# Holding four DMA transposes behind a load, and the next batch's loads behind the last transpose

## The chip, the cores and the metric

The kernel runs on one core of one Trainium2 chip. The metric is the device time of one execution in microseconds (us), and a kernel's figure is the median of its runs. "PE" is the tensor engine, "DVE" the vector engine, "ACT" the scalar engine, "POOL" and "SP" the two engines that issue the DMAs of this part.

## The reference, cut to what matters

Linear attention over 8 batches, whose result feeds a mixture of experts. Only the attention's first steps matter here:

```python
def phi(x, c, s):
    r = np.maximum(x, 0.0)
    return np.concatenate([r * c, r * s], axis=-1)
q_p = phi(q, cos_w, sin_w)                 # q, k, v: 8 batches, 8 heads, 576 x 64
k_p = phi(k, cos_w, sin_w)
kv = np.einsum('bhsf,bhsd->bhfd', k_p, v)  # summed over the sequence
z = np.sum(k_p, axis=2)
num = np.einsum('bhsf,bhfd->bhsd', q_p, kv)
den = np.einsum('bhsf,bhf->bhs', q_p, z)[..., None] + 1e-06
attn = num / den                           # then the experts: relu(x @ w1) @ w2, weighted
```

`q_p` must stand the other way round for its matmuls, so it is transposed. That is what the change is about.

## The kernel before

Block j runs the first expert's matmuls (`h_ps`, `y_ps`) on the j-th slice of 512 tokens and, between them, prepares later batches. Each batch's q, k and v come in six loads of 288 KB (two halves of each), issued by POOL. Heads go in four pairs. The q of batches 2 and up is multiplied by DVE into a buffer `q_p` and turned by a DMA transpose on SP's queue. Batches count from 0, so the fourth is `b == 3` and the fifth `b == 4`.

```python
te, ve, se = bound    # PE, DVE and ACT, each held to the order in which the program is written
qp_pool = p1.enter_context(tc.tile_pool(name="qp_pool", bufs=3))       # three buffers for q_p
...
def load(b, half, names="qkv", held_back=False):
    for name in names:
        x = ld.tile([P, 2, C, D], F16, name=f"{name}_ld")
        view = ...
        i = nc.gpsimd.dma_start(out=..., in_=view[:, 2 * half : 2 * half + 2])
        if held_back:
            after(ve.last, i)             # wait for DVE's last instruction so far
        landing[name, b, half] = i
...
def prep_q(b, hk):
    q16 = loaded.pop(("q", b, hk))
    by_dma = b >= 2
    if by_dma:
        ve.tensor_scalar(out=q16, in0=q16, scalar1=0.0, scalar2=None, op0=ALU.max)
    q_p = qp_pool.tile([P, C, 2, D], F16, name="q_p")
    ve.tensor_tensor(out=q_p[:], in0=..., in1=cs, op=ALU.mult)
    if by_dma:
        qTs[b, hk] = q_pTs[(b * HK + hk) % len(q_pTs)]
        turned = nc.sync.dma_start(out=qTs[b, hk], in_=..., transpose=True)
        if b == 3 and hk == 0:
            after(landing["v", b, 1], turned)
...
# block 1 prepares batch 3, block 2 batch 4; the numbers are slots of the block
(4, prep_q, 0), (5, prep_q, 1), (8, prep_k, 0), (8, prep_q, 2), ...    # j == 1
(4, prep_q, 0), (5, prep_k, 0), (5, prep_q, 1), (6, prep_k, 1),        # j == 2
(8, prep_q, 2), (8, prep_k, 2), (10, prep_q, 3), (10, prep_k, 3),
(11, prep_kv, 0), (14, prep_kv, 1),
...
if j == 1:
    for name in "qkv":
        for half in range(2):
            at(j, 12, load, b + 2, half, name, True)
```

(The comment lines are mine. In the last part `b` is j + 1, the batch whose attention block j finishes, so that block 1 prepares batch 3 and issues the loads of batch 4, the fifth, which block 2 prepares. `prep_k` is ACT's relu on k; `prep_kv` is DVE's multiplication into `k_p` and its copy of v.) The destinations of the four transposes are `q_pT`, `q_pT`, `acc_lo` and `acc_hi` in the profile, for pairs 0 to 3.

The softmax here doesn't subtract the row's maximum and nothing guards it: scores larger than these inputs give would overflow.

## Time and profile before

| before | value |
|---|---|
| median of 3 runs | 978.64 us (978.47 to 978.7) |
| span of the profiled run | 977.2 us |
| PE busy | 98% of the span |
| PE idle, 54.63 to 110.35 us | 2.00 us |
| fourth batch's transposes issued at | 54.33 (pair 1), 64.13 (0), 65.53 (2), 67.03 (3) |
| fifth batch's loads begin at | 66.92 us |

The timeline of SP's queue in the kernel before: start, length of the issuing, line, then output<-input and how many were grouped. A line with x2 or x4 covers that many transposes from the first one's start to the last one's issue; it is not their time in flight.

```profile
54.33 11.09 SPq L361 DMA_TRANSPOSE q_pT<-q_p  x2
65.53 1.32 SPq L361 DMA_TRANSPOSE acc_lo<-q_p  x1
67.03 1.48 SPq L361 DMA_TRANSPOSE acc_hi<-q_p  x1
77.75 7.20 SPq L361 DMA_TRANSPOSE q_pT<-q_p  x4
```

The first line holds pair 1 (54.33) and pair 0 (64.13, when v had landed). Then POOL's timeline in the same kernel, where the brackets say what ended POOL's wait:

```profile
66.92 1.43 POOL L202 DMA_DIRECT2D q_ld<-in_q_dram  x2 [11.63 <-DVE acc_lo L109]
```

The fifth batch's loads start a tenth of a microsecond before the transpose of pair 3 is issued at 67.03: these two meet.

### The profile page before, as it was taken

The numbers are of one execution on the slowest core, as the hardware profiler recorded it, in microseconds if no ns is written. First come the engines' busy times: TensorE is split into PE (matmuls) and PEld (weight loads), VectorE is DVE, ScalarE is ACT, GpSimd is POOL, SyncE is SP. The second block draws the span as 40 slices with busy tenths as digits, with TensorE's granted clock in tenths as the row PEclk, the third lists the DMA queues.
The fourth block names the chain that finished last, engine by engine and source line by source line (L and its number), as shares of the span: only waits on it lengthen the run. The fifth ranks groups of instructions, "written<-read, shape, count | busy, mean of one in ns | idle before, by whom it ended". The sixth has DMA issues, their size and how long they took to land.

```text
span 977.2 us, 20236 instructions
## 1 busy us (share of the span) xinstructions
PE 962.4 (98%) x7855; PEld 675.7 (69%) x7855; DVE 807.8 (83%) x1833; ACT 564.7 (58%) x1262; POOL 60.6 (6%) x82
## 2 busy tenths in 40 slices
PE   9999999999999999999999999999999999999997
PEld 6545555457777777777777777777777777777775
DVE  6767775888988887988888887988888888988887
ACT  5766665477776555555555555555555555555551
POOL 6231110010000000000000000000000000000001
PEclk9999999999999999999999999999999999999999
DMA  9999986330104401323104401323103401104435
GB/s 163 183 149 178 152 141 111 68 68 34 42 25 83 78 25 41 64 51 70 35 25 83 78 25 36 68 55 66 37 25 80 81 25 38 37 26 120 127 89 128
DMA packets 80336, 73.54 MB, mean 75 GB/s; under 512 B 33264, under 2 KB 72176, under 8 KB 80240
## 3 DMA queue, kind: packets, MB, share of 16 engines
q0 software_dynamic: 27232, 30.94, 20.3%
q1 hardware_dynamic: 52768, 41.06, 17.2%
q8 instruction: 61, 1.00, 0.4%
q14 instruction: 35, 0.29, 0.1%
q10 hardware_dynamic: 240, 0.26, 0.1%
HBM read 83.12 MB, written 12.98 MB: 98 GB/s over the span
## 4 chain that ended last, share of the span: by engine, by line
PE 88%; DMA 4%; DVE 3%; issue 2%; ACT 1%; POOL 1%; POOLq 0%; ACTq 0%; SPq 0%
PE rows_ps L109 33%; PE h_ps L109 26%; PE p_ps L109 11%; PE copied_ps L109 11%; PE y_ps L109 4%; PE small_ps L109 2%; DMA k_ld<-in_k_dram 1%; DMA w1e<-in_moe_w_dram 1%; DMA w2e<-in_moe_w_dram 1%; DMA acc_hi<-q_p 1%; DVE P_tok L109 1%; DVE colp L109 0%; POOL q_ld L202 0%; DVE rs L109 0%; DVE acc_hi L955 0%
## 5 line engine op out<-in xcount | busy, mean ns | idle before, releaser
L955 DVE SCALAR_TENSOR_TENSOR acc_lo<-rows_ps,P_tok,acc_lo 128x512 f32<-128x512 f32 (+1 forms) x322 | 203.9, 643 | 74.9 <-PE rows_ps L109 74.8
L109 PEld LDWEIGHTS <-H 128*128 128x128 f16 x2080 | 203.2, 98 | 82.5 <-issue 1.2
L891 ACT CAST u<-h_ps 128x384 f16<-128x384 f32 x288 | 138.0, 479 | 131.0 <-PE h_ps L109 131.0
L109 PEld LDWEIGHTS <-w1e 128*128 128x128 f16 x1632 | 157.7, 98 | 67.6 <-issue 5.3
L885 DVE CUSTOM_DVE_ANT_0 H<-p_ps,u 128x384 f16<-128x384 f32 x329 | 181.9, 553 | 6.5 <-PE p_ps L109 6.5
L109 PEld LDWEIGHTS <-hs 128*128 128x128 f16 x1500 | 146.6, 98 | 56.2
L109 PE MATMUL h_ps<-S,w1e 128*128 128x384 f16 x672 | 164.1, 326 | 0.7 <-ACT u L109 0.6
L109 PE MATMUL p_ps<-xT,T 128*128 128x384 f16 x672 | 164.1, 326 | 0.1
L109 PE MATMUL rows_ps<-V,H 128*128 128x256 f16 x1000 | 150.0, 273 | 0.7 <-DVE acc_hi L955 0.7
L109 PE MATMUL rows_ps<-w2e,hs 128*128 128x256 f16 x1000 | 150.0, 273 | 0.0
L109 PE MATMUL h_ps<-xT,w1e 128*128 128x384 f16 (+1 forms) x616 | 148.7, 350 | 0.1
L923 ACT ACTIVATE H<-h_ps 128x384 f16<-128x384 f32 x144 | 70.8, 492 | 95.0 <-PE h_ps L109 95.0
L109 PEld LDWEIGHTS <-T 128*128 128x128 f16 x1008 | 98.4, 98 | 30.2 <-issue 3.6
L109 PE MATMUL rows_ps<-w2e,H 128*128 128x256 f16 (+1 forms) x568 | 92.3, 285 | 0.0
L904 ACT COPY copied_ps<-h_ps 128x384 f32<-128x384 f32 x144 | 67.5, 469 | 35.4 <-PE h_ps L109 35.4
L914 ACT ACTIVATE H<-copied_ps 128x384 f16<-128x384 f32 x144 | 71.0, 493 | 20.3 <-PE copied_ps L109 20.3
L109 PE MATMUL h_ps<-S,T 128*128 128x384 f16 x336 | 81.8, 325 | 0.4 <-ACT copied_ps L109 0.3
L109 PE MATMUL copied_ps<-xT,w1e 128*128 128x384 f16 x336 | 82.1, 326 | 0.0
L109 PE MATMUL copied_ps<-w2e,H 128*128 128x256 f16 x504 | 75.5, 272 | 0.0
L109 PE MATMUL rows_ps<-V,hs 128*128 128x256 f16 x500 | 75.0, 272 | 0.0
L955 DVE SCALAR_TENSOR_TENSOR acc_lo<-copied_ps,P_tok,acc_lo 128x256 f32<-128x256 f32 x126 | 60.4, 480 | 0.6 <-PE copied_ps L109 0.2
L955 DVE SCALAR_TENSOR_TENSOR acc_hi<-rows_ps,P_tok,acc_hi 128x512 f32<-128x512 f32 (+1 forms) x56 | 41.4, 739 | 20.5 <-PE rows_ps L109 19.7
(145 smaller groups left out, 951.7 us busy)
## 6 DMA issues: line engine op xcount, KB each, us to landing
S<-x_saved SPq DMA_DIRECT2D x108, 192.0 KB, 2.4
out_dram<-acc_lo SPq DMA_DIRECT2D x62, 128.0 KB, 2.4
w1e<-in_moe_w_dram POOLq DMA_DIRECT2D x7, 1024.0 KB, 8.8
w2e<-in_moe_w_dram POOLq DMA_DIRECT2D x7, 1024.0 KB, 9.7
q_ld<-in_q_dram POOLq DMA_DIRECT2D x16, 288.0 KB, 7.1
k_ld<-in_k_dram POOLq DMA_DIRECT2D x16, 288.0 KB, 8.5
v_ld<-in_v_dram POOLq DMA_DIRECT2D x16, 288.0 KB, 9.6
x_saved<-S SPq DMA_DIRECT2D x18, 192.0 KB, 1.9
```

The costliest lines, as they stand in the source:

```text
L109: i = getattr(self.engine, name)(*args, **kwargs)
L885: latest = ve._custom_dve(TENSOR_ADD_SAT, out=out, in0=ps[:, 0:TU], in1=t[:], s0=FP32_MAX, s1=0.0)
L891: se.copy(out=t[:], in_=ps[:, 0:TU])
L904: se.copy(out=Y[:, 0:TU], in_=X[:, 0:TU])
L914: se.activation(out=h11, in_=Y[:, 0:TU], func=AF.Relu)
L923: se.activation(out=h12, in_=X[:, 0:TU], func=AF.Relu)
L955: ve.scalar_tensor_tensor(out=a, in0=rows, scalar=P_tok[:, g, self.e : self.e + 1], in1=a, op0=ALU.mult, op1=ALU.add,)
```

## The change

The intent: keep transposes and loads of one batch apart, and the next batch's loads off the last transpose. It also moves the fifth batch's k relus later, to leave the loads time.

```diff
-        def load(b, half, names="qkv", held_back=False):
+        def load(b, half, names="qkv", held_back=False, behind=None):
...
-                if held_back:
+                if behind is not None:
+                    after(turnings[behind], i)
+                elif held_back:
                     after(ve.last, i)
...
-                if b == 3 and hk == 0:
+                if b == 3:
                     after(landing["v", b, 1], turned)
+                turnings[b, hk] = turned
...
-                    (4, prep_q, 0), (5, prep_k, 0), (5, prep_q, 1), (6, prep_k, 1),
-                    (8, prep_q, 2), (8, prep_k, 2), (10, prep_q, 3), (10, prep_k, 3),
+                    (4, prep_q, 0), (5, prep_q, 1), (7, prep_k, 0), (8, prep_k, 1),
+                    (8, prep_q, 2), (9, prep_k, 2), (10, prep_q, 3), (10, prep_k, 3),
...
-                        at(j, 12, load, b + 2, half, name, True)
+                        at(j, 12, load, b + 2, half, name, True, (b + 1, HK - 1))
```

More of the change, by code (lines that the diff above doesn't have):

```diff
@@ L195 @@
         landing = {}
+        turnings = {}
         sources = {"q": q, "k": k, "v": v}
-        def load(b, half, names="qkv", held_back=False):
+        def load(b, half, names="qkv", held_back=False, behind=None):
             for name in names:
```

## The prediction

> **What bounds the kernel now.** I read the share of each engine first, then the slices, then the tensor engine's (PE's) waits in the stretch that the change touches, then the orders of time there.
>
> ```profile
> PE 962.4 (98%) x7855; PEld 675.7 (69%) x7855; DVE 807.8 (83%) x1833; ACT 564.7 (58%) x1262; POOL 60.6 (6%) x82
> ...
> PE   9999999999999999999999999999999999999997
> ```
>
> PE is busy 98% of the span and in nearly every slice, so a change counts only by what it adds to or takes from PE's idle time. The change touches the batches around 50 to 90 us. The table by stretches gives PE 17.30 us busy of the 19.30 us from 54.6 to 73.9, and no idle from 73.9 to 88. So about 2.0 us of idle time is all there is to win here, 0.2% of 978.64. PE's waits from 36 to 160 us name the larger pieces:
>
> ```profile
> PE small_ps L109 <- DMA acc_hi<-q_p: 1.0, 1, 1.0
> PE small_ps L109 <- ACT rb L109: 0.4, 1, 0.4
> PE small_ps L109 <- DVE acc_lo L109: 0.3, 1, 0.3
> PE small_ps L109 <- DVE k_p L109: 0.2, 1, 0.2
> ```
>
> The first is the fourth batch's last transpose (its q goes into acc_hi). It is what the change aims at. The timeline of PE shows the place, with the idle time in brackets:
>
> ```profile
> 68.43 0.46 PE L109 MATMUL small_ps<-acc_lo,k_p 64*128 64x65 f16 x18 [0.33 <-DVE acc_lo L109]
> 69.09 0.46 PE L109 MATMUL small_ps<-acc_lo,k_p 64*128 64x65 f16 x18 [0.21 <-DVE k_p L109]
> 69.48 2.76 PE L109 MATMUL h_ps<-xT,w1e 128*128 128x512 f16 x12
> 72.18 0.51 PE L109 MATMUL small_ps<-q_pT,zsel 128*32 128x192 f16 x12
> 72.52 0.34 PE L109 MATMUL small_ps<-acc_lo,zsel 128*32 128x192 f16 x6
> 73.81 0.34 PE L109 MATMUL small_ps<-acc_hi,zsel 128*32 128x192 f16 x6 [0.96 <-DMA acc_hi<-q_p]
> ```
>
> The reader is to see two things: the 0.96 us, and that the two waits just before it are for the vector engine (DVE), so at 68 to 69 us PE goes as DVE goes.
>
> **What the Trainium skill says.** "DMA: Bandwidth & Descriptors", section "Issuing engines are not separate DMA queues", says that transfers share the same 16 DMA engines and interleave, whoever issued them. This trace agrees: a transpose of 54.33 us, beside five loads, took 10.4 us to land; one of 64.13, just after the last of them landed, took 3.3; one of 67.03, beside the fifth batch's loads, took 6.7. The same page, section "Anatomy of one DMA", says that DMA engines do not wait on semaphores; the issuing sequencer does, before dispatch. So a wait holds up everything behind it on that queue; the trace shows the SP queue held 6.8 us in total by the v load. The same page's "Rules for kernel authors" says that a transpose next to ordinary DMAs needs nothing, so the new waits are for time alone.
>
> **The change, part by part.** The instruction lists of the two builds show the same order on PE and DVE in this stretch. Only three things differ.
>
> First, the order of the fourth batch's transposes. Before, only that of head pair 0 waited for the v load, so the scheduler put pair 1 ahead of it: pair 1 went at 54.33 among the loads, pair 0 at 64.13, when v landed. Now all four go after that landing, in the order 0, 1, 2, 3. The q_p pool has three buffers, so the multiplication that makes q_p of pair 3 must wait for the first finished transpose. DVE's wait is on the same semaphore lane in both builds, but that lane was pair 1's transpose and becomes pair 0's. Before:
>
> ```profile
> 63.83 0.30 DVE L109 TENSOR_SCALAR q_ld<-q_ld 128x576 f16<-128x576 f16 x1
> 64.82 0.76 DVE L109 TENSOR_TENSOR q_p<-q_ld,acc_hi 128x1152 f16<-128x1152 f16 x1 [0.70 <-DMA q_pT<-q_p]
> 65.50 0.75 DVE L109 TENSOR_TENSOR k_p<-k_ld,acc_hi 128x1152 f16<-128x1152 f16 x1
> 66.17 0.45 DVE L109 COPY acc_lo<-v_ld 128x576 f16<-128x576 f16 x1
> ```
>
> 54.33 + 10.4 = 64.7, and q_p starts at 64.82.
>
> When does it start now? The last v load was issued at 54.57 (the second of the two at 53.86, 0.72 later) and took 9.5 us: 64.1. Without the transpose among them the loads should finish earlier. Two undisturbed sets of six loads say how much: of those begun at 103.70 and 122.64 the fifth landed 11.6 and 11.1 us after the first issue; here five took 64.1 - 51.72 = 12.4. So I take 51.72 + 11.3 = 63.0 for v's landing. A transpose with no load beside it lands in 3.2 to 3.3 us even when others follow at once (those of 97.60, 99.00 and 100.44 did). So pair 0 lands at 63.0 + 0.1 + 3.3 = 66.4 and q_p of pair 3 starts at about 66.5, **1.7 us later** than 64.82.
>
> DVE keeps a fixed order, so the k_p and v copies behind it move by 1.7 us too. The second half of the key-value sums waited for exactly these (0.33 and 0.21 us above). So PE's restart at 69.48 moves to about 71.2. An earlier PE doesn't help: the new delay is set by v's landing.
>
> Second, the collision goes. q_p of pair 3 is done at about 67.2, its transpose goes at about 67.3 and, with the loads held back, lands at about 70.6. PE reaches it at about 72.8 + 1.7 = 74.5: no wait. This wins the 0.96 us.
>
> Third, the fifth batch's loads start at about 70.6 in place of 66.92, 3.7 us later. With the undisturbed spacing (5.2 us for the first, then about 1.5 each) they land at about 75.8, 77.3, 78.9, 80.4, 82.0 and 83.6, perhaps a microsecond later at the end, as that batch's own transposes come among them. Wanted: q first half by DVE at 76.60 + 0.7 = 77.3, second half at 79.3. The k relus on ACT took place from 77.25; the change puts them two or three slots later, at about 80.2 and 83, which is after 78.9 and 80.4. The v copies were at 84.20 and later, now about 84.9, after 82 to 83. So I expect these loads hidden. The moved relus free two h_ps evictions ahead of them but put 0.7 us before the second rb copy; there I allow 0 to 0.3 us of PE waiting.
>
> Sum: + 1.7 (DVE held by the buffer) - 0.96 (the collision) + 0 to 0.3 = about + 0.8; I take **+0.7 us**, as some of the DVE delay may be caught between two PE groups. 978.64 + 0.7 = 979.3. From 78 us on PE has no idle time of note up to the end of the attention part to absorb either sign, so I let it reach the end whole.
>
> **Rivals.** (a) *The collision is all that matters*: the transpose is ready in time, and q_p of pair 3 isn't late, as the v load comes far sooner without the transpose in its way. For it: k second half landed 3.0 us after k first half in before (57.8, 60.8), against about 1.5 in the undisturbed sets, so the transpose may have cost 1.5 us; v would land at 62.6, and if 62.0 the shift is 0.7 and the net -0.3. At best all 2.0 us of idle go: 976.7. Against it: the pool's buffer and 3.3 us of transpose stay. (b) *The late loads become the bound*: moved 3.7 us, with transposes among them as at 77.75 (5.0 us to land), one q, k or v misses its slot, holds DVE or ACT and then PE by 1 to 2 us: 980.5 to 981.5. For it: before, ACT already waited 0.53 us for k at 77.25. Against it: the relus were moved for this. (c) *No difference*: the wait for the transpose is exchanged for an equal one for DVE, 978.6.
>
> **Range and chances.** The term of the widest spread is v's landing, 62.0 to 64.1: the shift on DVE is then 0.7 to 2.8, the net -0.3 to +1.8. With rival (b) above it and a few tenths of spread between runs, 977.8 to 980.8 should hold 8 in 10, with the centre at 979.3. Two per cent is 19.6 us; even all the idle time of this stretch is 2.0, and no loads can be late by so much. So within 2% is near certain.
>
> **What would show it.** Right: the first transpose of the fourth batch goes at about 63 and lands 3.3 us later; DVE starts q_p of pair 3 at 66 to 67, with a wait of 2 us or more for the transpose; PE waits about 2 us in total for the k_p and v copies at 67 to 71 us; the wait for acc_hi is gone, and its transpose takes 3.3 in place of 6.7; the six loads start at about 70.6. Wrong: v lands before 62, so that DVE isn't later and the time falls below 978; or PE or ACT waits at 76 to 88 for q, k or v of the fifth batch or for rb, which would make it slower than said; or a later batch's order of transfers changes, which I take as unmoved but shifted.

## The result, and the profile after

| | before | after |
|---|---|---|
| median, 4 runs each | 978.56 us (977.54 to 978.7) | 980.23 us (979.34 to 981.58) |
| span of the profiled run | 977.2 us | 978.4 us |
| granted clock in it | 1.000 | 0.999 |

The ratio is 1.002, with a 95% interval of 1.0003 to 1.0038: within 2%, and a little slower.

PE's waits from 36 to 160 us in the changed kernel (what waited, for what: sum in us, times, longest):

```profile
PE small_ps L109 <- DVE acc_lo L109: 2.1, 3, 1.6
PE small_ps L109 <- ACT rb L109: 0.9, 1, 0.9
PE small_ps L109 <- DVE k_p L109: 0.2, 1, 0.2
```

The wait for `acc_hi`, 0.96 us before, is gone. In its place PE waits 2.1 us for DVE's v copies (`acc_lo`), where it waited 0.3. PE's timeline shows the place:

```profile
68.98 0.46 PE L109 MATMUL small_ps<-acc_lo,k_p 64*128 64x65 f16 x18 [1.62 <-DVE acc_lo L109]
...
70.74 0.46 PE L109 MATMUL small_ps<-acc_lo,k_p 64*128 64x65 f16 x18 [0.33 <-DVE acc_lo L109]
71.40 0.46 PE L109 MATMUL small_ps<-acc_lo,k_p 64*128 64x65 f16 x18 [0.21 <-DVE k_p L109]
71.79 2.76 PE L109 MATMUL h_ps<-xT,w1e 128*128 128x512 f16 x12
...
74.99 0.34 PE L109 MATMUL small_ps<-acc_hi,zsel 128*32 128x192 f16 x6
75.26 1.90 PE L109 MATMUL h_ps<-xT,w1e 128*128 128x512 f16 x8
```

The first line is the new idle time, 1.62 us. The group at 71.79 is the one that started at 69.48 before, so PE is 2.31 us late here. The `acc_hi` group at 74.99 follows without a wait, which gives 0.96 back and a little more: the group at 75.26 started at 74.09 before, so 1.17 us stays. That is nearly the whole difference of the two spans, 1.2 us. DVE's timeline says why PE waited:

```profile
67.14 0.76 DVE L109 TENSOR_TENSOR q_p<-q_ld,acc_hi 128x1152 f16<-128x1152 f16 x1 [2.44 <-DMA q_pT<-q_p]
67.81 0.75 DVE L109 TENSOR_TENSOR k_p<-k_ld,acc_hi 128x1152 f16<-128x1152 f16 x1
68.48 0.45 DVE L109 COPY acc_lo<-v_ld 128x576 f16<-128x576 f16 x1
```

DVE stood still for 2.44 us before it could fill the last `q_p`: the first line's bracket names a transpose. Its k_p and v follow in the written order, and PE's idle time ends when the first v copy is done. SP's queue shows the transposes that DVE waited for:

```profile
63.73 2.73 SPq L365 DMA_TRANSPOSE q_pT<-q_p  x2
66.56 1.35 SPq L365 DMA_TRANSPOSE acc_lo<-q_p  x1
68.08 1.28 SPq L365 DMA_TRANSPOSE acc_hi<-q_p  x1
78.93 9.18 SPq L365 DMA_TRANSPOSE q_pT<-q_p  x4
```

All four now go after v's landing; each of them landed 3.2 to 3.3 us after its issue, where that of `acc_hi` took 6.7 before. The last line holds the fifth batch's four, which took 7.0, 6.7, 5.4 and 4.3 us to land, against 5.0, 4.9, 3.8 and 4.9 before. POOL's line is the gate at work, 4.9 us after where the loads started before:

```profile
71.83 1.43 POOL L203 DMA_DIRECT2D q_ld<-in_q_dram  x2 [16.48 <-DMA acc_hi<-q_p]
```

One more measure helps from here on, because single runs spread by more than the effect. Every build issues the same PE instructions in the same order, so I take two of them, the last `h_ps` group before 55 us and an `h_ps` pair at about 110 us, and call the time between them the stretch. PE's idle time in it is the stretch less PE's busy time there. For the changed kernel the stretch is 57.16 us, of which 53.80 busy and 3.36 idle; before it is 55.72, of which 53.72 busy and 2.00 idle. After the stretch the changed kernel is shorter, 866.54 us against 866.87. The idle time leaves out a little of each wait: the `h_ps` matmul before a wait is counted as busy for its whole 0.38 us, where the next one otherwise starts 0.22 us after it. So the stretch is the safer of the two measures.

### The profile page after: what moved, and what is told of

The parts are those of the page before. It is cut to its first block, busy times and chain, and to the rows that moved or that the text cites. A ratio compares the mean times of both kernels' runs of the same rounds, so it can differ in the third digit from the quotient of the medians.

```text
span 978.4 us, 20236 instructions
## 1 busy us (share of the span) xinstructions
PE 962.3 (98%) x7855; PEld 675.6 (69%) x7855; DVE 807.7 (83%) x1833; ACT 564.3 (58%) x1262; POOL 60.6 (6%) x82
## 4 chain that ended last, share of the span: by engine, by line
PE 88%; DMA 4%; DVE 4%; issue 2%; ACT 1%; POOL 1%; POOLq 0%; DVEq 0%; ACTq 0%; SPq 0%
PE rows_ps L109 33%; PE h_ps L109 26%; PE p_ps L109 11%; PE copied_ps L109 11%; PE y_ps L109 4%; PE small_ps L109 2%; DMA k_ld<-in_k_dram 1%; DMA w2e<-in_moe_w_dram 1%; DMA w1e<-in_moe_w_dram 1%; DVE P_tok L109 1%; DVE k_p L109 0%; DVE colp L109 0%; DVE acc_lo L109 0%; DMA q_pT<-q_p 0%; DVE xT L109 0%
```

## The experiments

Theory A, my prediction's: the change wins the collision's 0.96 us and pays for it with DVE, which the three `q_p` buffers hold until the first transpose has landed. Rival B: the late loads cost time later on. The prediction's rival (a), that the collision is all that matters, is already out: the changed kernel's trace has no collision, and it isn't faster. The experiments ran in three sets of four kernels, each set on one chip; every set has 11 runs of the kernel before, with medians 979.82, 978.86 and 978.94 us.

| kernel | median (range), us | ratio to before [95%] | stretch | PE idle in it |
|---|---|---|---|---|
| the change, first runs | 980.23 (979.34–981.58) | 1.0020 [1.0003, 1.0038] | 57.16 | 3.36 |
| e1 change again | 979.87 (979.44–981.04) | 0.9999 [0.9977, 1.0021] | 56.60 | 2.65 |
| e9 change, third time | 980.68 (978.99–980.86) | 1.0010 [0.9998, 1.0022] | 57.88 | 3.71 |
| e5 before again | 978.53 (977.62–979.38) | 0.9994 [0.9979, 1.0008] | 55.67 | 1.98 |
| e2 loads gated only | 979.38 (979.00–980.07) | 0.9992 [0.9972, 1.0011] | 57.52 | 3.41 |
| e3 transposes wait only | 978.68 (978.15–979.26) | 0.9984 [0.9965, 1.0004] | 57.36 | 2.48 |
| e4 change, four buffers | 986.81 (985.53–989.58) | 1.0069 [1.0047, 1.0091] | 65.04 | 9.67 |
| e6 e2, k relus later | 979.18 (978.85–981.25) | 1.0005 [0.9989, 1.0020] | 56.70 | 2.79 |
| e7 e6, other k relu later too | 980.22 (979.69–980.73) | 1.0011 [0.9996, 1.0025] | 57.86 | 3.88 |
| e8 before, one k relu later | 978.22 (977.91–981.53) | 0.9997 [0.9980, 1.0014] | 55.15 | 1.49 |
| e10 change, k relus not moved | 980.92 (979.72–983.16) | 1.0021 [1.0008, 1.0034] | 60.79 | 4.81 |
| e11 loads behind pair 2 | 978.04 (976.57–978.87) | 0.9985 [0.9973, 0.9997] | 55.49 | 1.31 |
| e12 e11, one k relu later | 977.98 (977.51–979.06) | 0.9989 [0.9977, 1.0000] | 56.47 | 2.51 |

### e1 and e9: the change again

No edit.

> The changed kernel once more, with five rounds, to fix the size of the difference. Theory A (the wait of q_p's third buffer for the first transpose holds DVE, and PE behind it, for about 2.2 us, and 1.0 us is won back from the collision): slower by 1.0 to 1.5 us, as the profiled PE waits say (3.07 against 1.87 us). Rival C (the difference of the two medians, 1.7 us, is chance between runs): within 0.5 us of the kernel before.

> The changed kernel a third time, beside the kernel before on the same chip, since the second set left the size open (the kernel before had several runs at a lower clock there). From the traces, PE takes 55.7 us in the kernel before and 56.6 to 57.2 in the changed one between the same two of its instructions (its last h_ps group before 55 us and the pair at 110 us), and as long in both for all the rest. Expected: slower by 0.8 to 1.5 us in the medians. If the difference were chance: within 0.3 us.

In e1 the median is the same as before's, 979.87 against 979.82, though the trace is like the first one: PE waits 1.58, 0.33 and 0.21 us for DVE, and the stretch is 0.9 us longer than the 55.7 of the kernel before. The kernel before lost runs in this set: four of its eleven took 981.2 to 984.2 us. So the ratio of that set says little, and I read e1 from its trace. In e9, on another chip, the medians differ by 1.7 us, and a second cost appears. DVE's timeline, then PE's, of e9:

```profile
86.62 0.76 DVE L109 TENSOR_TENSOR q_p<-q_ld,acc_hi 128x1152 f16<-128x1152 f16 x1 [4.02 <-DMA q_pT<-q_p]
```

```profile
88.92 0.38 PE L109 MATMUL h_ps<-xT,w1e 128*128 128x512 f16 x1 [0.89 <-DVE xT L109]
89.65 0.59 PE L109 MATMUL h_ps<-xT,w1e 128*128 128x512 f16 x2 [0.35 <-DVE xT L109]
```

DVE waited 4.02 us for the fifth batch's first transpose, again for a `q_p` buffer, and PE waited 1.24 us for DVE's `xT` behind it. In the first trace the same wait of DVE was 2.33 us and cost PE nothing. This is rival B, in a form that I hadn't named: not a late load, but late loads that now run beside the fifth batch's transposes.

### e2: only the loads wait

```diff
-                if b == 3:
+                if b == 3 and hk == 0:
```

> Only the fifth batch's loads wait for the last transpose; of the fourth batch's transposes only the first waits for v, as in the kernel before (so the scheduler puts the second ahead again). Theory A: DVE isn't held (q_p of pair 3 at about 64.8), the last transpose lands in 3.3 us, PE's wait for it (0.96 us) is gone: faster than the kernel before by 0.9 to 1.1 us. Rival B (it is the late start of the fifth batch's loads that costs): still slower than the kernel before by about 1 us, as the loads still start some 3.5 us later.

The first half came as expected: the last transpose took 3.2 us, PE didn't wait for it, and DVE filled the last `q_p` at 64.82 after a wait of 0.73 us, where it had been 0.70 before. But the gain was lost: 3.41 us idle in place of 2.00. Part of it is 1.24 us for `rb` at 59.37, a wait that comes and goes (e5 below). The rest is in ACT's timeline and in PE's:

```profile
79.60 0.68 ACT L109 ACTIVATE k_ld<-k_ld 128x576 f16<-128x576 f16 x1 [1.40 <-DMA k_ld<-in_k_dram]
```

```profile
80.70 0.49 PE L109 MATMUL small_ps<-q_pT,kv_sb 128*64 128x384 f16 x4 [1.13 <-ACT rb L109]
```

ACT waited 1.40 us for k, the `rb` copy stood behind that relu, and PE waited 1.13 us for `rb`. The loads had started at 70.82. So theory A's number for this run, faster by the collision's microsecond, missed, although its reading of DVE held: gating the loads behind the last transpose costs later about what it wins, and that is rival B.

### e3: only the transposes wait

```diff
-                        at(j, 12, load, b + 2, half, name, True, (b + 1, HK - 1))
+                        at(j, 12, load, b + 2, half, name, True)
```

> All of the fourth batch's transposes wait for v, and the fifth batch's loads go when they did before (after DVE's last work). Theory A: the same DVE hold of about 2.3 us as with the whole change, so slower than the kernel before by 1.0 to 1.5 us; the last transpose and the loads collide again (over 5 us to land), but PE, late by 2.3 us, comes to it at about 75 and waits little, 0 to 0.5 us. Rival B: the loads aren't late, so no slower than the kernel before, within 0.3 us.

Here DVE's hold is alone (2.62 us before `q_p` at 65.54, PE waiting 1.79 and 0.30), and I expected the collision to stay on top of it. It didn't: the transpose of pair 3, issued at 66.56, landed in 3.3 us, as the loads started only at 67.64. They wait for a DVE copy, and DVE was late. So once all four transposes wait for v, the gate on the loads has nothing left to prevent; it only makes them later. The fifth batch's transposes took 3.2 to 4.2 us here, against 4.3 to 7.0 in the change. The time is 1.2 us under that of e1 in the same set, and not above that of the kernel before (0.9984). So theory A's number, slower by 1.0 to 1.5 us, missed, and rival B's, no slower, came true, though DVE's hold is in the trace as theory A has it.

The profiled run of e3 lost something else. PE's timeline, then the table by stretches, whose columns are the stretch, its length, then the engines' busy times in the order PE, PEld (weight loads), DVE, ACT and POOL with counts, the granted clock, the DMA share and GB/s:

```profile
67.39 0.46 PE L109 MATMUL small_ps<-acc_lo,k_p 64*128 64x65 f16 x18 [1.79 <-DVE acc_lo L109]
...
69.15 1.34 PE L109 MATMUL small_ps<-acc_lo,k_p 64*128 64x65 f16 x36 [0.30 <-DVE acc_lo L109]
70.42 3.56 PE L109 MATMUL h_ps<-xT,w1e 128*128 128x512 f16 x12
```

```profile
67.00:68.00 1.00, 0.61 (x19) 0.54 (x20) 1.00 (x4) 0.13 (x1) 0.36 (x1) 1.00 1.00 189
68.00:69.00 1.00, 0.84 (x4) 0.20 (x2) 1.00 (x3) 0.36 (x3) 1.00 (x2) 0.83 1.10 207
...
70.00:71.00 1.00, 1.00 (x20) 0.61 (x15) 0.20 (x3) 0.43 (x2) 1.00 (x2) 0.50 1.14 128
...
73.00:74.00 1.00, 1.00 (x8) 0.34 (x9) 0.00 (x0) 0.60 (x1) 0.00 (x0) 1.00 1.20 204
```

The clock fell to 0.50 at about 68.7, 1.3 us after the gap of 1.79 us had ended and before that of 0.30, and stayed there for about 3.4 us (0.83 in the stretch from 68 to 69, 0.50 from 69 to 72). The twelve matmuls at 70.42 took 3.56 us, where the same group took 2.76. The Trainium skill ("TensorE: Matmul & The Clock Gate", Part 1) says that the clock is halved after an idle window of about 3.4 us, and that this window is free-running. The trace agrees on the half, and the clock stayed halved for 3.4 us here and again in e10. It differs on the idle time: one gap of 1.79 us came before the fall here, and gaps of 1.18 and 0.67 us in e10, while the changed kernel's like gaps, 1.62 and 0.33 us, and one of 1.87 us in e7 left the clock at 1.00. What decides it is not shown.

### e4: the change with four q_p buffers

```diff
-        qp_pool = p1.enter_context(tc.tile_pool(name="qp_pool", bufs=3))
+        qp_pool = p1.enter_context(tc.tile_pool(name="qp_pool", bufs=4))
...
-        rb_pool = p1.enter_context(tc.tile_pool(name="rb_pool", bufs=4))
+        rb_pool = p1.enter_context(tc.tile_pool(name="rb_pool", bufs=3))
```

The second edit frees the memory for the first.

> The whole change, with a fourth q_p buffer (its space is taken from the rb pool, three buffers in place of four). Theory A: DVE's wait of 2.44 us for the transpose is gone, PE doesn't wait for the v copies for 1.62 us, and the collision is gone too: faster than the kernel before by 0.7 to 1.5 us, and than the changed one by about 2 us or more. Rival B: as slow as the changed kernel.

The table by stretches for 64 to 74 us, e4 and then the change:

```profile
64.00:74.00 10.00, 10.00 (x136) 5.02 (x134) 6.55 (x17) 6.09 (x15) 3.24 (x5) 1.00 0.79 137
```

```profile
64.00:74.00 10.00, 7.85 (x105) 3.92 (x104) 5.55 (x15) 5.11 (x13) 2.17 (x4) 1.00 0.71 125
```

PE is busy 10.00 us of 10 where in the change it is 7.85, with the transposes still waiting for v. So DVE's hold in the change is the buffer's, as theory A has it. But the time missed what was expected: the whole is 7 us slower than e1, from a place that nobody had asked about. PE's timeline of e4:

```profile
94.06 0.34 PE L109 MATMUL small_ps<-q_pT,zsel 128*32 128x192 f16 x6 [1.31 <-DMA q_pT<-q_p]
101.04 0.51 PE L109 MATMUL small_ps<-q_pT,zsel 128*32 128x192 f16 x6 [6.64 <-DMA q_pT<-q_p]
```

PE waits 8.0 us for the fifth batch's transposes, which took 8.7, 6.9, 10.5 and 15.5 us. In e4 DVE doesn't wait for a buffer at 81.17 either, so the sixth batch's loads, which wait for DVE, start at 83.27 in place of 88.11, among those transposes. The three buffers had held the loads back. That is shown by these traces for e4; what `rb`'s smaller pool adds wasn't tried alone (PE's waits for `rb` are 1.6 us there).

### e5 and e8: the kernel before again, and with one relu moved

e5 has no edit. e8, against before, moves one k relu of the fourth batch a slot on (and another with it):

```diff
-                    (4, prep_q, 0), (5, prep_q, 1), (8, prep_k, 0), (8, prep_q, 2),
-                    (9, prep_k, 1), (10, prep_kv, 0), (10, prep_k, 2), (12, prep_q, 3),
+                    (4, prep_q, 0), (5, prep_q, 1), (8, prep_q, 2), (9, prep_k, 0),
+                    (10, prep_k, 1), (10, prep_kv, 0), (10, prep_k, 2), (12, prep_q, 3),
```

> The kernel before against itself, to see how far it spreads and whether its slow runs have a cause in the trace. In the last set its runs went from 977.9 to 984.2 us, those above 981 all with a mean granted clock of 0.998. Theory D (short idle gaps of PE close together now and then make the throttle halve PE's clock for some 3.4 us, which costs about 1.7 us; seen once, in the run with the transposes' waits alone): again two clusters, 978 and about 2 us above, with lower mean clock in the upper one; ratio within 0.997 to 1.003. Rival (chip or order of runs): one cluster, or clusters that the clock doesn't tell apart.

> The kernel before with nothing but the fourth batch's first k relu one slot later. It takes the rb wait at 59 us away (0.4 us in the first trace). Expected: 0 to 0.5 us faster than before in its lower cluster, since from 64 us on the last transpose's landing (67.03 + 6.7) sets PE's restart and PE would only come to it earlier. If the rb wait counted in full: 0.4 to 1.2 us faster.

e5 has the waits of the kernel before: 0.92 us for `acc_hi`, whose transpose took 6.7 us again, and 0.91 for `rb` (0.4 in the first trace). So the wait for `acc_hi` repeats, and that for `rb` differs by half a microsecond between two traces of one kernel. Theory D's two clusters did not come again: e5's five runs lie within 1.8 us. Of all runs of the kernel before in the three sets, the six above 981 us had a mean clock of 0.998, but 979.69 and 979.38 us came with 0.997. No trace of one of the six was kept, so what makes them slow stays open. e8 takes the `rb` wait away and shortens the stretch by 0.5 us. The ratio, 0.9997 with an interval of 0.0034, can't confirm so little.

### e6, e7 and e12: moving relus out of the way

e6 is e2 with the fifth batch's k relus a slot later; e7 adds e8's edit to e6; e12 adds it to e11.

```diff
-                    (4, prep_q, 0), (5, prep_q, 1), (7, prep_k, 0), (8, prep_k, 1),
-                    (8, prep_q, 2), (9, prep_k, 2), (10, prep_q, 3), (10, prep_k, 3),
+                    (4, prep_q, 0), (5, prep_q, 1), (8, prep_q, 2), (8, prep_k, 0),
+                    (9, prep_k, 1), (10, prep_q, 3), (10, prep_k, 2), (10, prep_k, 3),
```

> Only the fifth batch's loads wait (as in the second experiment), but the fifth batch's k relus on ACT go one slot later still, behind the second pair's rb copies. In the second experiment PE waited 1.13 us there for rb, because ACT had waited 1.40 us for k. If the late loads were what ate the gain there: this wait is below 0.3 us, and the time is 0.8 to 1.2 us below the second experiment's, near 978.3. If not: the same as the second experiment, about 979.4.

> As the sixth, and the fourth batch's first k relu goes one slot later as well, behind the rb copies of its own slot, since PE waited 0.4 to 1.2 us for rb at 59 us whenever k landed late. Expected: that wait is 0 to 0.2 us; in all PE waits 0.6 to 0.9 us from 36 to 165 us, against 1.9 in the kernel before, and the time is 977.0 to 978.0, faster than both kernels. It fails if the k and v work that now comes later holds the sums at 66 to 70 us.

> The eleventh with the fourth batch's first k relu one slot later (as in the eighth, where it shortened the stretch by 0.5 us). Expected: 0.8 to 1.4 us below the kernel before; if the two gains don't add up, because DVE then sets the restart at 69 us, about as the eighth alone, 0.5 us below.

e6 and e7 missed their times. In e6 ACT waited 0.23 us for k in place of 1.40 and PE's second `rb` wait was gone, but DVE then waited 4.70 us for the fifth batch's first transpose (9.0 us in flight), and PE 1.62 and 0.35 us for `xT`. In e7 it was 4.95 on DVE and 1.87 and 0.35 on PE; in e12 4.07, and 0.94 and 0.35. The late loads overlap the fifth batch's transposes, and an earlier PE only meets them sooner. The median of e12 is 0.96 us below that of the kernel before in its set, inside the 0.8 to 1.4 expected, and its trace is that of the slowest of its five runs (979.06); but it is level with e11's (977.98 against 978.04), so that the gains of e8 and e11 add is not shown.

### e10: the change without the moved relus

```diff
-                    (4, prep_q, 0), (5, prep_q, 1), (7, prep_k, 0), (8, prep_k, 1),
-                    (8, prep_q, 2), (9, prep_k, 2), (10, prep_q, 3), (10, prep_k, 3),
+                    (4, prep_q, 0), (5, prep_k, 0), (5, prep_q, 1), (6, prep_k, 1),
+                    (8, prep_q, 2), (8, prep_k, 2), (10, prep_q, 3), (10, prep_k, 3),
```

> The change without its third part: the fifth batch's k relus stay where they were. The loads start at about 71.8, so k lands at about 80, and ACT asks for it at about 78.4 ahead of the h_ps evictions. If the moved relus are what hides the late loads: ACT waits about 2 us for k, PE 1 to 2 us behind it, 1 to 2 us slower than the whole change. If the late loads would be hidden anyway: the same as the change.

ACT's timeline:

```profile
79.80 0.68 ACT L109 ACTIVATE k_ld<-k_ld 128x576 f16<-128x576 f16 x1 [3.16 <-DMA k_ld<-in_k_dram]
```

ACT waited 3.16 us for k, held two `hT` behind it, and PE waited 1.18 and 0.67 us for these. So the moved relus are worth 1.85 us of PE waiting in this trace. The medians differ by 0.24 us from e9's, where 1 to 2 us were expected, with ranges that overlap; how much of the 1.85 a usual run keeps stays open. The profiled run was the slowest of its six: after these two gaps its clock was 0.50 for 3.4 us from 83.5 (0.86 in the mean from 84 to 94 us).

### e11: release the loads one transpose sooner

Pair 3's transpose is the last; here the loads wait for that of pair 2, and only pair 0 waits for v, as before.

```diff
-                if b == 3:
+                if b == 3 and hk == 0:
...
-                        at(j, 12, load, b + 2, half, name, True, (b + 1, HK - 1))
+                        at(j, 12, load, b + 2, half, name, True, (b + 1, HK - 2))
```

> The fifth batch's loads wait for the fourth batch's third transpose, not the last (and only its first transpose waits for v). The loads then start at about 69 in place of 66.9 (before) or 71.8 (change), when the last transpose is already under way. Theory (a transpose slows only by the loads' packets beside it, and each microsecond of delay of the loads comes back in the fifth batch's transposes): the last transpose lands in 3.3 to 4.5 us, PE's wait for it is 0 to 0.3 us, the fifth batch's transposes are only a little slower than before (5 to 6 us), and the time is 0.3 to 0.9 us below the kernel before. If any delay of the loads costs what it wins: the same as before.

POOL's timeline, then PE's:

```profile
69.14 1.43 POOL L203 DMA_DIRECT2D q_ld<-in_q_dram  x2 [14.26 <-DMA acc_lo<-q_p]
```

```profile
68.08 0.46 PE L109 MATMUL small_ps<-acc_lo,k_p 64*128 64x65 f16 x18 [0.33 <-DVE acc_lo L109]
...
72.34 0.34 PE L109 MATMUL small_ps<-acc_hi,zsel 128*32 128x192 f16 x6
72.60 1.90 PE L109 MATMUL h_ps<-xT,w1e 128*128 128x512 f16 x8
```

The loads start at 69.14, and pair 3's transpose, issued at 66.69, had 2.4 of its 3.2 us behind it: PE takes `acc_hi` at 72.34 without a wait. The loads are 1.7 us earlier than in e2, so ACT waits 0.24 us for k, PE doesn't wait for a second `rb`, and DVE's 2.90 us wait for the fifth batch's first transpose stays hidden. That batch's transposes took 7.6, 7.0, 5.3 and 4.3 us, the first two more than the 5 to 6 expected. PE's idle time falls to 1.31 us. The medians are below both: 978.04 us against 978.94 for before in the same set (0.9985, interval 0.9973 to 0.9997), and 980.68 for the change (e9). The interval only just leaves out 1, in one of thirteen comparisons, and the trace gains 0.2 us in the stretch and 0.27 after it; so the gain over the change is clear, that over the kernel before is likely.

## Why the prediction was right

It said 979.3 us in a range of 977.8 to 980.8, and within 2%. The first four runs gave 980.23; the other two sets of the change 979.87 and 980.68. The waits that it named are in the traces, and its first two terms hold in the mean; the third was too small, and the sum with it. They can be checked one by one.

- **DVE held by the buffer, +1.7 us.** `q_p` started at 67.14 in place of 64.82, 2.3 us later, in the first trace. Counted from the stretch's start it begins at 12.5, 11.6 and 11.5 us in the three traces of the change, and at 10.2 and 10.1 in the two of before: 1.7 us later in the mean, as predicted. The term was built from v landing 11.3 us after the issue of the first of the last five loads. The three traces of the change, taking the first transpose's issue as v's landing, give 63.73 − 51.79 = 11.9, then 11.3 (e1) and 11.0 (e9), so 11.3 was a fair middle and the first trace a late one. The 3.3 us of the transpose were right. e4 confirms the cause: with a fourth buffer (and one `rb` buffer fewer) PE has no idle time there.
- **The collision, −0.96 us.** Right in each trace of the change: no wait for `acc_hi`, and 3.2 us in place of 6.7 in the first. e3 adds what I had missed: the first part of the change would have done that alone, because it makes the loads late through DVE.
- **The late loads, 0 to +0.3 us.** They started at 71.83, not 70.6. Of the 1.2 us, 0.6 come from the later `q_p`; the loads began 0.5 us after the last transpose's landing at 71.3, which I had taken as at once; the small rest is the transpose's start. q, k and v came in time in the first trace, as I said: ACT's first k relu at 80.39 had no wait. The step that failed is "with transposes among them as at 77.75 (5.0 us to land)". Two of these took 7.0 and 6.7 us, in e9 one took 8.9, and there they cost PE 1.24 us.
- **How the loss divides.** I cut the stretch in two at the `h_ps` group behind `acc_hi` (74.09 in before). Up to it the change takes 20.59, 19.68 and 19.63 us, before 19.46 and 19.33: 0.57 more in the mean, where the first two terms together said 0.74. From it on the change takes 36.56, 36.93 and 38.25 us, before 36.26 and 36.35: 0.3 to 2.0 more, 0.94 in the mean, where 0 to 0.3 was allowed. So rival (b), which I kept out of the sum, is the larger part of the loss in e1 and e9. The other runs agree: this second part takes 37.1 to 39.2 us in e2, e6, e7, e11 and e12, whose loads wait for a transpose (e4 and e10, with further losses there, take more), and 36.2 to 36.5 in e3 and e8, whose loads don't.
- **The sum, +0.7 us.** The stretch was 57.16, 56.60 and 57.88 us in the three traces of the change, 57.2 in the mean, and 55.72 and 55.67 in the two of before: +1.5 us, of which 1.25 is PE's idle time. The rest of the program is 0.27 us shorter, so about +1.25. That rest is 866.54 to 866.62 us in all nine profiled runs with three `q_p` buffers in which the fifth batch's relus were moved, and 866.82 to 866.87 in the four without. The small gain goes with the third part of the change; why it arises after 110 us I didn't look into. I hadn't foreseen it, and it makes up for some of the late loads' cost, so that the number came as near as it did is partly luck.

Rival (a) fell with the changed kernel's own trace. Rival (c), an even exchange, is what the medians of e1's set show, but not the traces: the stretch and PE's idle time grew in all three. The size to a tenth stays open: the ratios 1.002, 0.9999 and 1.001 overlap, and runs of one kernel spread by 1 to 6 us. I hadn't foreseen the halved clock after short gaps; whether it makes that spread is not shown.

## What to carry to other kernels

Before you make a transfer wait so that it doesn't collide, ask which buffer it frees and which engine, held to a fixed order, stands behind that buffer; the wait passes through it to everything that follows. Hold a transfer back only until the collision is mostly over: one transpose sooner (e11) was faster than the full gate, which moved the collision into the next batch. And a buffer that seems too few may be what paces the loads: the fourth one (with one `rb` buffer fewer) made this kernel 7 us slower.

## What the Trainium skill lacked or had wrong

- "Advanced Engine Details and Errata", section "X-Bar Transpose (TRN2)", says that transpose DMAs are as fast as regular ones. By itself a transpose of 128 x 1152 f16, 288 KB, landed in 3.2 to 3.5 us here, with the next issued every 1.4 to 1.5 us, and none of the loads of this size after 40 us landed sooner than 4.2 us; so these runs don't speak against it. But beside loads a transpose took up to 10.4 us in the kernel before, and 15.5 in e4. Neither that page nor "DMA: Bandwidth & Descriptors" says how much a transpose slows beside plain loads. The loads lost far less: from the issue of the first of the fourth batch's last five loads to v's landing it took 11.9 to 13.3 us in the eight traces with a transpose among them, and 11.0 to 11.9 in the six without.
- "TensorE: Matmul & The Clock Gate", Part 1, ties the halved clock to an idle window of about 3.4 us. It also tells of a kernel whose short idles between groups of matmuls made the clock go up and down, but not how much idle time that takes. In e3 one gap of 1.79 us sufficed, and in e10 two of 1.18 and 0.67 us within 2.2 us; 1.62, 0.33 and 0.21 us in the changed kernel's first trace didn't, nor did 1.87 and 0.35 us in e7.
